# Attention and mixture of experts on one core: weight sums and a remainder moved to other places of the schedule, a scratch tile of their own, some copies on ScalarE

## The chip, the cores and the metric

The program runs on one core of one Trainium2 chip. The metric is the device time of one execution in microseconds (us); medians and ranges are over the executions of a job. TensorE is called PE in the profile, VectorE DVE, ScalarE ACT, GpSimd POOL, SyncE SP; "SPq" rows are transfers that the sync engine issues. The time in such a row is that of the issue; the data land later (tile 1's outputs 3.3 to 3.9 us after their issue in the changed kernel).

## The reference

```python
# q, k, v: (batch 8, heads 8, positions 576, 64)
scores = 1 / np.sqrt(64) * np.matmul(q, k.transpose(0, 1, 3, 2))
ret = scores * Dmat                     # gamma_h ** (i - j) for i >= j, else 0
attn = np.matmul(ret, v)
x = attn.transpose(0, 2, 1, 3).reshape(4608, 512)
p = domain_probs / (domain_probs.sum(-1, keepdims=True) + 1e-09)
for e in range(4):                      # w1[e]: 512 x 1024, w2[e]: 1024 x 512
    out += p[:, e:e+1] * (np.maximum(x @ w1[e], 0) @ w2[e])
```

## The kernel before

The 4608 tokens are worked in nine tiles of 512. A batch has 576 positions: four chunks of 128 and a remainder of 64. Tile 0 uses ordinary matmuls for x @ w1; from tile 1, expert 1 on, a "fast" product takes seven block products in place of eight, and for this it needs sums of weight blocks (per expert) and sums of token blocks (per tile). Attention of the next batches is woven into the same instruction streams.

Weight sums, all on VectorE, with two scratch tiles out of the ring `tmp`, which the token sums on GpSimd use too:

```python
def weight_sums(e):
    s = ssum[e] = wpool.tile([128, 3, 2, HF], BF16, tag=f"ws_{e}", name="wsum")
    ...
    for kc in range(2):
        def first(...):
            t[1] = tpool.tile([128, HF], FP32, tag="tmp", name="tmp")
            nc.vector.tensor_tensor(t[1], a21, a22, op=ADD)
        def second(...):
            t[2] = tpool.tile([128, HF], FP32, tag="tmp", name="tmp")
            nc.vector.tensor_tensor(t[2], t[1], a11, op=SUB)
        jobs += [first, second,
                 lambda ...: nc.vector.tensor_copy(s[:, 0, kc], t[1]),
                 lambda ...: nc.vector.tensor_copy(s[:, 1, kc], t[2]),
                 lambda ...: nc.vector.tensor_tensor(s[:, 2, kc], a12, t[2], op=SUB)]
        late.append(...)        # a21 <- a11 - a21, in place
```

Tile 0 is a list of 56 numbered groups of matmuls; `at(g, ...)` puts work behind group g in program order (T: transposes of queries and keys, S: scores, O: attention outputs, x: their copies into the token tile):

```python
at(39, T(0) of batch 1); at(40, S(0), masks); ...; at(47, O(3), x(3))      # shortened
at(48, narrow, lambda: [f() for f in token_sums(1)],
       lambda: [a1().cast_rem(n, nc.gpsimd) for n in "kqv"])
at(50, lambda: a1().Trem())
at(52, lambda: (a1().Srem(), a1().Srem_mask()))
at(54, lambda: (a1().Orem(), a1().x(NCH, nc.vector)))
sums_at(1, 17); sums_late(1, 22); sums_at(0, 23)
sums_at(2, 33); sums_late(2, 38); sums_at(3, 48); sums_late(3, 53)
for g in range(49, 56):
    at(g, lambda: pool(1, 2))           # two GpSimd items of batch 2 and later
```

From then on a loop over tiles and experts emits `up_fast` twice for each expert. It has four gaps each time, and a gap takes four matmuls of the second product, up to two GpSimd items and one TensorE item of the attention chain. The output tiles `acc` are four buffers, so tile 2's first expert writes (on ScalarE) where tile 1's outputs have to be gone; and all input loads, transposes and outputs are issued by the sync engine in program order:

```python
apool = tc.tile_pool(name="apool", bufs=NSUB)                              # NSUB = 4
def evacuate(po, ns, cols):
    if e == 0:
        nc.scalar.activation(a, po, Copy, scale=pe)
    else:
        nc.vector.scalar_tensor_tensor(a, po, pe, a, op0=MULT, op1=ADD)
    if e == E - 1:
        eng = nc.scalar if cols.start else nc.sync
        eng.dma_start(out=out[...], in_=a)
...
# in the chain of batch b, after its remainder's casts:
add("POOL", lambda: (load_chunk(b + 1, 2), load_chunk(b + 1, 3), load_rem(b + 1)))
```

## Time and profile before

| | before |
|---|---|
| time, median (lowest to highest) | 559.34 us (558.02 to 560.03) |
| TensorE busy | 535.0 us of 558.7 |
| two long TensorE waits | 6.8 and 4.75 us |
| first fast product starts at | 108.37 us |

The page of the kernel before: busy time, the granted clock of TensorE in tenths in 40 slices of the span, and the chain that ended last. Apart from the first and the last slice, TensorE is under 90% busy only in slices 5 to 8, 56 to 112 us.

```profile
span 558.7 us, 10485 instructions
...
PE 535.0 (96%) x4133; PEld 334.5 (60%) x4206; DVE 266.3 (48%) x427; ACT 251.6 (45%) x450; POOL 225.9 (40%) x321
...
PE   8999876799999999999999999999999999999997
...
PEclk9999979799999999999999999999999999999999
...
PE 91%; DVE 5%; issue 1%; POOL 1%; DMA 1%; SPq 0%; POOLq 0%; DVEq 0%
```

The waits of TensorE, longest first in total: who waited, for whom, total, times, longest.

```profile
PE ptr L306 <- POOL qrb L275: 6.8, 1, 6.8
PE s L315 <- DVE qkT L298: 4.8, 1, 4.8
```

The first stall, in the timeline of the kernel before (start, duration, engine, line, operation; in brackets the idle time and what ended it). VectorE works off weight sums of expert 2 before it copies the transposed tile, and TensorE waits for that copy. The first line is the same operation as the second, at a time when GpSimd is idle. (Four of expert 2's sums here, under GpSimd's casts, took 1.2 to 1.5 us, the others 0.4 to 1.0.)

```profile
50.89 0.41 DVE L553 CAST wsum<-tmp 128x512 bf16<-128x512 f32 x1
...
62.04 1.29 DVE L553 CAST wsum<-tmp 128x512 bf16<-128x512 f32 x1
...
65.76 1.53 DVE L546 TENSOR_TENSOR tmp<-wt 128x512 f32<-128x512 bf16 x1
...
70.34 2.01 DVE L556 TENSOR_TENSOR wt<-wt 128x512 bf16<-128x512 bf16 x2
72.27 0.41 DVE L298 COPY qkT<-ptc 128x512 bf16<-128x512 bf16 x1
72.73 0.61 PE L315 MATMUL s<-qkT 64*128 64x128 bf16 x8 [4.75 <-DVE qkT L298]
```

The second stall. GpSimd idles for 15.69 us, then works off the token sums of tile 1 and only after them casts the remainder of batch 1.

```profile
91.55 1.15 POOL L566 TENSOR_TENSOR tmp<-xT 128x512 f32<-128x512 bf16 x1 [15.69 <-DVE xT L233]
...
98.88 1.48 POOL L275 TENSOR_TENSOR qrb<-raw_qr,gq 64x512 bf16<-64x512 f32 x1
...
100.42 0.39 PE L306 MATMUL ptr<-ident,qrb 64*128 64x64 bf16 x4 [6.80 <-POOL qrb L275]
```

And the clock after each of them, in stretches of 2 us: stretch, busy time of each engine, granted clock, mean share of the DMA engines, GB/s. The clock is at half while TensorE works again; by the stretches after these it is full at about 77.9 and 105.2 us, that is 5.2 and 4.8 us after the work begins.

```profile
72.00:74.00 2.00, 1.27 (x17) 0.77 (x17) 1.26 (x3) 0.26 (x1) 2.00 (x3) 0.50 1.02 213
74.00:76.00 2.00, 2.00 (x11) 1.14 (x10) 0.72 (x3) 0.94 (x3) 0.86 (x2) 0.50 0.93 168
...
102.00:104.00 2.00, 1.79 (x5) 0.67 (x5) 2.00 (x2) 0.60 (x1) 2.00 (x3) 0.50 0.53 125
```

### The profile page before, as it was taken

The page shows a single profiled execution, that of the slowest core. Times are in us where ns is not written, and L with a number is a line of the kernel's source. Part 1 is how long each engine was busy: PE and PEld are TensorE (multiplying, and loading weights), DVE is VectorE, ACT ScalarE, POOL GpSimd, SP SyncE. Part 2 cuts the span into 40 slices and gives each one's busy share as a digit, 9 for nine tenths or more (in the row PEclk, how much of TensorE's full clock was granted, in tenths as well). Part 3 has the DMA queues.
Part 4 walks back from the last instruction along what each step waited for, and adds up shares of the span by engine and source line. Part 5 has one row for each costly group of instructions (what it writes and reads, how often), then busy time and mean ns, then how long its engine had stood idle before and what let it go on. Part 6 is the DMA issues. An engine that isn't in the chain of part 4 may idle for free.

```text
span 558.7 us, 10485 instructions
## 1 busy us (share of the span) xinstructions
PE 535.0 (96%) x4133; PEld 334.5 (60%) x4206; DVE 266.3 (48%) x427; ACT 251.6 (45%) x450; POOL 225.9 (40%) x321
## 2 busy tenths in 40 slices
PE   8999876799999999999999999999999999999997
PEld 3644443466666666666666666666666666666664
DVE  6618864945554455434443545344524442443343
ACT  3453232264445544454446344644464446445541
POOL 6601534947928836842264635510510320100000
PEclk9999979799999999999999999999999999999999
DMA  9999995589399396595028901200100010001002
GB/s 237 194 205 200 215 205 90 142 154 168 57 178 200 78 186 91 131 192 81 2 95 141 170 11 76 49 1 1 73 5 0 2 76 1 0 17 61 2 1 76
DMA packets 148817, 53.98 MB, mean 97 GB/s; under 512 B 130684, under 2 KB 143228, under 8 KB 148768
## 3 DMA queue, kind: packets, MB, share of 16 engines
q1 hardware_dynamic: 141296, 44.79, 40.0%
q0 software_dynamic: 7328, 8.39, 8.9%
q8 instruction: 33, 0.54, 0.4%
q14 instruction: 16, 0.13, 0.1%
q10 hardware_dynamic: 144, 0.13, 0.1%
HBM read 45.16 MB, written 9.44 MB: 98 GB/s over the span
## 4 chain that ended last, share of the span: by engine, by line
PE 91%; DVE 5%; issue 1%; POOL 1%; DMA 1%; SPq 0%; POOLq 0%; DVEq 0%
PE po L519 43%; PE upP L583 20%; PE upR L583 10%; PE ph L478 5%; PE upQ L583 5%; PE oc L356 2%; PE s L315 2%; PE kvp L326 1%; PE oc L359 1%; DVE wt L556 1%; DMA raw_q<-in_q_dram 1%; DVE wsum L555 0%; PE warm_out L153 0%; DVE acc L509 0%; DVE xT L233 0%
## 5 line engine op out<-in xcount | busy, mean ns | idle before, releaser
L519 PE MATMUL po<-wt,hT 128*128 128x512 bf16 (+1 forms) x1093 | 278.7, 377 | 3.6 <-issue 0.3
L519 PEld LDWEIGHTS <-hT 128*128 128x128 bf16 x1160 | 113.2, 98 | 81.3
L604 POOL TENSOR_SCALAR hT<-hT 128x512 bf16<-128x512 bf16 x62 | 38.1, 614 | 211.5 <-DVE hT L603 210.7
L509 DVE SCALAR_TENSOR_TENSOR acc<-po,probs,acc 128x512 f32<-128x512 f32 (+1 forms) x109 | 80.9, 742 | 79.0 <-PE po L519 75.3
L583 PEld LDWEIGHTS <-wt 128*128 128x128 bf16 x992 | 91.3, 98 | 35.9 <-issue 0.2
L595 DVE TENSOR_TENSOR upR<-upP,m 128x512 f32<-128x512 f32 x62 | 43.4, 699 | 126.9 <-PE upP L583 126.9
L583 PEld LDWEIGHTS <-wsum 128*128 128x128 bf16 x744 | 72.6, 98 | 21.1
L583 PE MATMUL upP<-tsum,wt 128*128 128x256 bf16 x496 | 74.8, 273 | 0.1
L603 DVE TENSOR_TENSOR hT<-upP,m 128x512 bf16<-128x512 f32 x62 | 42.9, 692 | 55.7 <-PE upP L583 54.2
L598 ACT ACTIVATE hT<-upQ 128x512 bf16<-128x512 f32 x62 | 37.0, 597 | 69.1 <-PE upQ L583 69.1
L608 ACT ACTIVATE hT<-upR 128x512 bf16<-128x512 f32 x62 | 37.0, 597 | 54.3 <-PE upR L583 54.3
L612 ACT ACTIVATE hT<-upP 128x512 bf16<-128x512 f32 x62 | 37.0, 597 | 48.7 <-PE upP L583 47.1
L589 ACT ACTIVATE upQ<-upP 128x512 f32<-128x512 f32 x62 | 36.1, 583 | 46.2 <-PE upP L583 46.1
L320 DVE TENSOR_TENSOR sT<-s,tri 128x512 bf16<-128x512 f32 x56 | 37.9, 682 | 9.3 <-PE s L315 9.3
L494 ACT ACTIVATE hT<-ph 128x512 bf16<-128x512 f32 x40 | 23.5, 597 | 41.6 <-PE ph L478 40.8
L478 PE MATMUL ph<-xT,wt 128*128 128x512 bf16 (+3 forms) x174 | 39.7, 377 | 0.6 <-issue 0.4
L583 PE MATMUL upP<-xT,wt 128*128 128x256 bf16 x248 | 37.4, 273 | 0.0
L583 PE MATMUL upQ<-xT,wt 128*128 128x256 bf16 x248 | 37.2, 273 | 0.0
L583 PE MATMUL upP<-tsum,wsum 128*128 128x256 bf16 x248 | 37.2, 273 | 0.0
L583 PE MATMUL upR<-xT,wsum 128*128 128x256 bf16 x248 | 37.2, 273 | 0.0
L583 PE MATMUL upR<-tsum,wsum 128*128 128x256 bf16 x248 | 37.2, 273 | 0.0
L591 ACT ACTIVATE m<-upR 128x512 f32<-128x512 f32 x62 | 36.7, 592 | 0.0
(110 smaller groups left out, 457.5 us busy)
## 6 DMA issues: line engine op xcount, KB each, us to landing
out_dram<-acc SPq DMA_DIRECT2D x35, 256.0 KB, 2.1
raw_k<-in_k_dram SPq DMA_DIRECT2D x32, 256.0 KB, 4.8
raw_q<-in_q_dram SPq DMA_DIRECT2D x32, 256.0 KB, 5.1
raw_v<-in_v_dram SPq DMA_DIRECT2D x32, 256.0 KB, 5.2
wt<-in_moe_w_dram POOLq DMA_DIRECT2D x6, 1024.0 KB, 25.2
wt<-in_moe_w_dram POOLq DMA_DIRECT2D x4, 512.0 KB, 6.8
raw_kr<-in_k_dram SPq DMA_DIRECT2D x8, 128.0 KB, 5.1
raw_qr<-in_q_dram SPq DMA_DIRECT2D x8, 128.0 KB, 4.6
```

The source lines that it names most:

```text
L320: nc.vector.tensor_tensor(self.sT[c][:, j], self.s[c][j], tri[:, :].unsqueeze(1).to_broadcast([128, NP, C]), op=MULT)
L478: nc.tensor.matmul(ph[:, ts], lhsT=w1_sb[e][:, dc, fc * 128:(fc + 1) * 128], rhs=xts[nt][:, dc, ts], start=(dc == 0), stop=(dc == NDC - 1))
L509: nc.vector.scalar_tensor_tensor(a, po, pe, a, op0=MULT, op1=ADD)
L519: nc.tensor.matmul(po, lhsT=hT[:, fc, ns * 128:(ns + 1) * 128], rhs=w2_sb[e][:, fc, d:d + w], start=(fc == 0), stop=(fc == NFC - 1))
L583: nc.tensor.matmul(ps[:, l], lhsT=wa(kc)[:, f:f + 128], rhs=xa(kc), start=(start and l == 0 and kc == 0), stop=(kc == 1), skip_group_check ...
L591: nc.scalar.activation(m5, R_, Copy)
L595: nc.vector.tensor_tensor(R_, P, m5, op=ADD)
L598: nc.scalar.activation(hT[:, lo, t0], Q, Relu)
L603: nc.vector.tensor_tensor(h22, P, m5, op=ADD)
L604: nc.gpsimd.tensor_scalar(h22, h22, float("inf"), 0.0, op0=MIN, op1=MAX)
L608: nc.scalar.activation(hT[:, lo, t1], R_, Relu)
L612: nc.scalar.activation(hT[:, hi, t0], P, Relu)
```

## The change

The intent is to take both stalls away: expert 2's sums where VectorE has time, the remainder's casts where GpSimd idles, and the remainder's matmuls and half of expert 3's sums in the fast loop of tile 1. The weight sums get a scratch tile of their own, worked in place, and for experts 0 and 1 ScalarE makes the copies. Batch 2's chain now has to wait for the remainder of batch 1 (`first`). The diff, cut to its core (left out are the new places of the sums of experts 0 and 1, the queue `extra` for the other half of expert 3's, and a move of batch 0's last remainder step from group 36 to 34):

```diff
+        def copy(o, i):
+            if e < 2:
+                nc.scalar.activation(o, i, Copy)
+            else:
+                nc.vector.tensor_copy(o, i)
...
+            t = tpool.tile([128, HF], FP32, tag="wsum", name="wt", bufs=1)
...
+                nc.vector.tensor_tensor(t, a21, a22, op=ADD)
+                copy(s[:, 0, kc], t)
...
-            add("POOL", lambda: A.cast_rem("k", g), **({"PE": P} if n else {}))
+            add("POOL", lambda: A.cast_rem("k", g), **({"PE": P} if n else {"first": 1}))
...
-                add("PE", lambda: A.S(c), DVE=V + v, ACT=X + x, later=(b, c))
+                add("PE", lambda: A.S(c), DVE=V + v, ACT=X + x, later=(b, c), **({} if n else {"first": 2}))
...
+                elif k == "first":
+                    ok = len(rem1) < n
...
-    at(48, narrow, lambda: [f() for f in token_sums(1)], lambda: [a1().cast_rem(n, nc.gpsimd) for n in "kqv"])
-    at(50, lambda: a1().Trem())
-    at(52, lambda: (a1().Srem(), a1().Srem_mask()))
-    at(54, lambda: (a1().Orem(), a1().x(NCH, nc.vector)))
+    at(46, lambda: [a1().cast_rem(n, nc.gpsimd) for n in "kqv"])
+    at(48, narrow, lambda: [f() for f in token_sums(1)])
+    rem1 = {3: lambda: a1().Trem(), 5: lambda: (a1().Srem(), a1().Srem_mask()),
+            7: lambda: (a1().Orem(), a1().x(NCH, nc.vector))}     # by gap of the loop
...
-    sums_at(2, 33)
-    sums_late(2, 38)
-    sums_at(3, 48)
-    sums_late(3, 53)
+    sums_at(2, 26, 27, 28, 30, 31, 32)
+    sums_late(2, 33, 34)
+    sums_at(3, 48, 50, 52)              # the other half goes into the loop's windows
     for g in range(49, 56):
-        at(g, lambda: pool(1, 2))
+        at(g, lambda: pool(1, 1))
```

More of the change, by code (lines that the diff above doesn't have):

```diff
@@ L541, in weight_sums, with second @@
             a11, a12, a21, a22 = w[:, kc, :HF], w[:, 2 + kc, :HF], w[:, kc, HF:], w[:, 2 + kc, HF:]
-            t = {}
+            t = tpool.tile([128, HF], FP32, tag="wsum", name="wt", bufs=1)
             def first(kc=kc, a21=a21, a22=a22, t=t):
-                t[1] = tpool.tile([128, HF], FP32, tag="tmp", name="tmp")
-                nc.vector.tensor_tensor(t[1], a21, a22, op=ADD)
-            def second(a11=a11, t=t):
-                t[2] = tpool.tile([128, HF], FP32, tag="tmp", name="tmp")
-                nc.vector.tensor_tensor(t[2], t[1], a11, op=SUB)
-            jobs += [first, second,
-                     lambda kc=kc, t=t: nc.vector.tensor_copy(s[:, 0, kc], t[1]),
-                     lambda kc=kc, t=t: nc.vector.tensor_copy(s[:, 1, kc], t[2]),
-                     lambda kc=kc, t=t, a12=a12: nc.vector.tensor_tensor(s[:, 2, kc], a12, t[2], op=SUB)]
+                nc.vector.tensor_tensor(t, a21, a22, op=ADD)
+                copy(s[:, 0, kc], t)
+            def second(kc=kc, a11=a11, t=t):
+                nc.vector.tensor_tensor(t, t, a11, op=SUB)
+                copy(s[:, 1, kc], t)
+            jobs += [first, second, lambda kc=kc, t=t, a12=a12: nc.vector.tensor_tensor(s[:, 2, kc], a12, t, op=SUB)]
             late.append(lambda a11=a11, a21=a21: nc.vector.tensor_tensor(a21, a11, a21, op=SUB))
@@ L793 @@
     at(31, a0.Srem, a0.Srem_mask)
-    at(36, a0.Orem, lambda: a0.x(NCH, nc.vector))
+    at(34, a0.Orem, lambda: a0.x(NCH, nc.vector))
     at(25, begin1)
@@ L806, in narrow, with sums_at, sums_late @@
         turn.update(at=0)
-    at(48, narrow, lambda: [f() for f in token_sums(1)], lambda: [a1().cast_rem(n, nc.gpsimd) for n in "kqv"])
-    at(50, lambda: a1().Trem())
-    at(52, lambda: (a1().Srem(), a1().Srem_mask()))
-    at(54, lambda: (a1().Orem(), a1().x(NCH, nc.vector)))
+    at(46, lambda: [a1().cast_rem(n, nc.gpsimd) for n in "kqv"])
+    at(48, narrow, lambda: [f() for f in token_sums(1)])
+    rem1 = {3: lambda: a1().Trem(), 5: lambda: (a1().Srem(), a1().Srem_mask()),
+            7: lambda: (a1().Orem(), a1().x(NCH, nc.vector))}
     late = {}
-    def sums_at(e, g, n=2):
+    def sums_at(e, *gs):
         def start():
             state["jobs"], late[e] = weight_sums(e)
-        at(g, start)
-        for i in range(10):
-            at(g + i // n, lambda i=i: state["jobs"][i]())
-    def sums_late(e, g):
-        at(g, lambda: [f() for f in late[e]])
-    sums_at(1, 17)
-    sums_late(1, 22)
-    sums_at(0, 23)
-    sums_at(2, 33)
-    sums_late(2, 38)
-    sums_at(3, 48)
-    sums_late(3, 53)
+            extra.extend(state["jobs"][len(gs):])
+        at(gs[0], start)
+        for i, g in enumerate(gs):
+            at(g, lambda i=i: state["jobs"][i]())
+    def sums_late(e, *gs):
+        for i, g in enumerate(gs):
+            at(g, lambda i=i: late[e][i]())
+    sums_at(1, 16, 17, 17, 18, 19, 19)
+    sums_late(1, 20, 20)
+    sums_at(0, 20, 21, 21, 22, 23, 24)
+    sums_at(2, 26, 27, 28, 30, 31, 32)
+    sums_late(2, 33, 34)
+    sums_at(3, 48, 50, 52)
     for g in range(49, 56):
-        at(g, lambda: pool(1, 2))
+        at(g, lambda: pool(1, 1))
     head += [up_classical(0, 1), down_groups(0, 0), down_groups(0, 1), up_classical(0, 2), down_groups(0, 2),
@@ L847 @@
     turn.update(po=0)
-    extra += late[0]
-    before = (1, 0)
+    extra += late[3] + late[0]
+    before, gaps = (1, 0), 0
     for nt, e in [(nt, e) for nt in range(1, n_nt) for e in range(E)][1:]:
@@ L857, in gap @@
         def gap():
+            nonlocal gaps
+            gaps += 1
             for _ in range(4):
@@ L863, in gap @@
             pool(nt, 2)
+            rem1.pop(gaps, int)()
             chain.emit("PE", nt)
@@ L881 @@
             front.pop(0)()
+        while len(extra) > {(1, 1): 9, (1, 2): 9, (1, 3): 2}.get((nt, e), 0):
+            extra.pop(0)()
         for g in range(2):
```

## The prediction

> **What bounds the kernel.** TensorE: busy 535.0 of 558.7 us (96%, busy table), and the chain of waits is 91% TensorE. After about 112 us it is busy 99% (stretch table), so nothing is to be won there. Its idle time sits in two stalls of the first 110 us (waits of TensorE):
>
> 1. 4.75 us, 67.98 to 72.73 us: the first score matmuls of batch 1 wait for VectorE's copy of the transposed queries. VectorE has these weight sums of expert 2 queued ahead of the copy, from 60.05 us on (timeline), mixed with evacuations. They take 1.2 to 1.5 us each there, against 0.4 to 0.7 us at 49 to 55 us, because GpSimd casts batch 1 at the same time. (The Trainium skill, "SBUF — State Buffer", "Who interferes with whom", says such a VectorE instruction and a GpSimd one block each other; this trace agrees, with those numbers.)
> 2. 6.80 us, 93.6 to 100.42 us: the transposes of batch 1's remainder wait for GpSimd, which casts it (97.88 to 100.36) only after the token sums of tile 1 (91.55 to 97.9). GpSimd was idle from 75.9 to 91.5.
>
> Each stall drops the clock to 0.50 for about 5 us (granted clock by stretch; 128x512 matmuls go from 0.216 to 0.43 us apart). The Trainium skill, "TensorE: Matmul & The Clock Gate", "Part 1: The HAM clock gate", names both the half rate and the recovery after about 3.4 us of work; here it took nearer 5. That costs about 2.5 us per stall. A further 0.5 us is a wait for the remainder's mask at 107 us.
>
> **What the change does.** TensorE's work is the same, in another order.
> - Expert 2's sums move forward to 50-57 us, where VectorE has no evacuations and GpSimd is nearly idle. The first stall goes.
> - The remainder is cast before the token sums, in GpSimd's idle time, and its matmuls move into the gaps of tile 1's fast loop. The second stall goes; the token sums hide behind about 7 us of expert 0's matmuls.
> - Eight copies (0.4-0.8 us) of experts 0 and 1 go to ScalarE, which is 45% busy; the in-place scratch tile frees the sums from the token sums' tile (two 2.7 us VectorE waits).
> - Batch 2's scores begin four gaps later. Replaying the schedule, tile 2's token sums are still emitted about three gaps (5 us) before they are needed.
>
> **The sum.** Stalls 4.75 + 6.80 + 0.5 = 12.0; clock about 4.7; total 16.7. As a cross-check, the stretch 67.98-79.66 holds about 4.5 us of matmuls at full clock and 93.6-108.37 about 5.3, the same total. Costs that I expect: expert 0's second copy stands ahead of an activation evacuation on ScalarE while VectorE is late, at about 51 us (0.3-1 us); in tile 1's first fast group, expert 3's sums delay one VectorE addition (about 0.6 us, slowed by GpSimd). So 559.3 - 16.7 + 1.4 = 544.0 us. Range 540.5 to 548.0. Faster by over 2%: 0.91; within 2%: 0.08; slower: 0.01.
>
> **What would show it.** No TensorE wait over 1.5 us between 25 and 115 us; granted clock 1.00 there; TensorE busy about 530 us (fewer half-rate matmuls); expert 2's sums at about 0.7 us each; the first fast group starts near 92 us instead of 108.4; GpSimd casts the remainder at about 76-80 us.
>
> **What would make it wrong.** A new stall over about 3 us would drop the clock again: ScalarE blocked behind a weight-sum copy near 51 us, expert 3's sums with GpSimd's token sums and casts at 84-100 us, or GpSimd's late clamp of hT in tile 1 (my slack: about 6 us). Or batch 1's casts, paced by DMA until 76 us, become the next limit once stall 1 is gone (slack 1-3 us).

## The result, and the profile after

The changed kernel took 550.79 us (median of 4, 550.58 to 552.11) beside 559.68 us for the kernel before (558.02 to 560.78): a ratio of 0.9849, 95% interval 0.9819 to 0.9878. That is faster, but by 1.5%, outside the range. (A ratio is the mean time of one kernel's fast runs over that of the other's of the same rounds, so it is not quite the ratio of the medians.)

The page of the changed kernel. The low digits of slices 5 to 8 are gone; new ones stand in the twelfth and thirteenth slices.

```profile
span 548.9 us, 10483 instructions
...
PE 531.3 (97%) x4133; PEld 332.9 (61%) x4206; DVE 259.0 (47%) x419; ACT 255.7 (47%) x458; POOL 224.1 (41%) x321
...
PE   7999999999978999999999999999999999999997
...
PEclk9999999999997999999999999999999999999999
...
PE 92%; DVE 2%; DMA 2%; issue 1%; POOL 1%; SPq 0%; ACT 0%; DVEq 0%; ACTq 0%
```

The longest wait of TensorE in the changed kernel, and the longest that is left between 25 and 115 us:

```profile
PE upP L587 <- ACT upQ L593: 5.7, 1, 5.7
...
PE ph L478 <- ACT hT L494: 0.4, 1, 0.4
```

Up to there the forecast came true. Expert 2's sums run in GpSimd's quiet time at 0.43 to 0.71 us, and the remainder is cast from 76.2 us on. The first fast product starts at 89.75 us in place of 108.37 us. In the timeline of the changed kernel:

```profile
50.49 0.43 DVE L544 CAST wsum<-wt 128x512 bf16<-128x512 f32 x1
...
66.14 0.43 DVE L298 COPY qkT<-ptc 128x512 bf16<-128x512 bf16 x1 [2.92 <-PE ptc L296]
...
76.20 1.04 POOL L275 TENSOR_TENSOR krb<-raw_kr,gk 64x512 bf16<-64x512 f32 x1
...
89.75 0.60 PE L587 MATMUL upP<-xT,wt 128*128 128x256 bf16 x4
```

The kernel is thus 18.6 us ahead at the start of the loop. But from there to the end it takes 459.15 us (548.9 - 89.75) where the kernel before took 450.3 (558.7 - 108.37). About 0.8 us of the 8.8 is the remainder's matmuls, which moved into the loop. The rest is a new stall at 161 us and the half clock after it. The timeline of the changed kernel there, VectorE first (it finishes the second and the last output block of tile 1), then the sync queue, ScalarE and TensorE:

```profile
143.27 0.75 DVE L509 SCALAR_TENSOR_TENSOR acc<-po,probs,acc 128x512 f32<-128x512 f32 x1 [1.53 <-PE po L519]
...
151.02 0.75 DVE L509 SCALAR_TENSOR_TENSOR acc<-po,probs,acc 128x512 f32<-128x512 f32 x1 [1.00 <-PE po L519]
...
151.37 1.77 SPq L512 DMA_DIRECT2D out_dram<-acc  x1
153.19 0.43 SPq L109 DMA_DIRECT2D raw_k<-in_k_dram  x1
...
160.90 1.25 SPq L123 DMA_DIRECT2D raw_vr<-in_v_dram  x2
162.25 1.51 SPq L512 DMA_DIRECT2D out_dram<-acc  x3
...
165.62 0.69 ACT L507 ACTIVATE acc<-po,probs 128x512 f32<-128x512 f32 x1 [6.90 <-DMA out_dram<-acc]
166.21 0.59 ACT L593 ACTIVATE upQ<-upP 128x512 f32<-128x512 f32 x1
...
166.85 1.01 PE L587 MATMUL upP<-tsum,wsum 128*128 128x256 bf16 x4 [5.72 <-ACT upQ L593]
```

Read from below: TensorE waits for ScalarE to empty an accumulator bank; ScalarE stands before an earlier instruction, which writes tile 2's second `acc` buffer; that buffer still holds tile 1's second output block. VectorE had finished that block at 144.0 us (143.27 + 0.75), but its transfer left at 162.25 us, because the input loads of batch 4 stood ahead of it in the sync queue. Of these 18.2 us the last ten loads are 9.0; the rest is the first six loads, two transposes and tile 1's first output, which stay ahead of it in the runs defer and half too. The wait list names only ScalarE; one has to go two steps up to find a transfer. And the clock follows; it is full again at about 171.5 us, so it costs about 2.3 us:

```profile
166.00:168.00 2.00, 1.15 (x6) 0.82 (x6) 0.03 (x1) 1.31 (x3) 0.00 (x0) 0.50 0.88 163
168.00:170.00 2.00, 2.00 (x8) 0.75 (x6) 1.26 (x2) 0.60 (x1) 0.00 (x0) 0.50 0.52 104
```

In the kernel before the same loads also stood ahead of tile 1's outputs, but they started 7.35 us before VectorE took up tile 1's last block (162.86 against 170.21) and the last of them was issued 1.9 us after that block was done (172.84 against 170.96); in the changed kernel they start 2.2 us after it (153.19 against 151.02). Before, ScalarE had a wait for an output too, and TensorE none for it:

```profile
162.86 0.58 SPq L109 DMA_DIRECT2D raw_k<-in_k_dram  x1
...
170.21 0.75 DVE L509 SCALAR_TENSOR_TENSOR acc<-po,probs,acc 128x512 f32<-128x512 f32 x1 [1.01 <-PE po L519]
...
172.93 1.51 SPq L512 DMA_DIRECT2D out_dram<-acc  x3
...
175.79 0.69 ACT L507 ACTIVATE acc<-po,probs 128x512 f32<-128x512 f32 x1 [1.86 <-DMA out_dram<-acc]
```

### The profile page after: what moved, and what is told of

The parts are those of the page before. It is cut to its first block, busy times and chain, and to the rows that moved or that the text cites. A ratio compares the mean times of both kernels' runs of the same rounds, so it can differ in the third digit from the quotient of the medians.

```text
span 548.9 us, 10483 instructions
## 1 busy us (share of the span) xinstructions
PE 531.3 (97%) x4133; PEld 332.9 (61%) x4206; DVE 259.0 (47%) x419; ACT 255.7 (47%) x458; POOL 224.1 (41%) x321
## 4 chain that ended last, share of the span: by engine, by line
PE 92%; DVE 2%; DMA 2%; issue 1%; POOL 1%; SPq 0%; ACT 0%; DVEq 0%; ACTq 0%
PE po L519 43%; PE upP L587 20%; PE upR L587 10%; PE ph L478 6%; PE upQ L587 5%; PE oc L356 2%; PE s L315 2%; DMA raw_q<-in_q_dram 1%; PE oc L359 1%; PE kvp L326 1%; DVE sT L447 1%; DMA out_dram<-acc 1%; POOL km L267 0%; PE ptc L296 0%; DVE qm L398 0%
## 5 line engine op out<-in xcount | busy, mean ns | idle before, releaser
L478 PE MATMUL ph<-xT,wt 128*128 128x512 bf16 (+3 forms) x175 | 35.8, 355 | 0.6 <-ACT hT L494 0.4
L267 POOL TENSOR_TENSOR km<-raw_k,gk 128x512 bf16<-128x512 f32 x28 | 30.2, 1078 | 12.0 <-DMA raw_k<-in_k_dram 9.3
```

Source lines behind the costliest of these rows:

```text
L478: nc.tensor.matmul(ph[:, ts], lhsT=w1_sb[e][:, dc, fc * 128:(fc + 1) * 128], rhs=xts[nt][:, dc, ts], start=(dc == 0), stop=(dc == NDC - 1))
```

## The experiments

Theory A: the outputs wait in the sync queue behind batch 4's loads, since batch 2's chain, and with it every later load, now lags four gaps further behind the loop. Rival B: the DMA engines are simply full there, wherever the output stands. Rival C: the wait is only labelled so. Rival D: the earlier start of the loop alone brings the stall about, with either half of the change. Eleven runs were made, of nine new kernels (again is the changed kernel, defer5 is defer once more), all with correct results. Each job ran the kernel before on the same chip; the medians of before were 558.81, 559.52 and 558.69 us for the three jobs.

### outq: outputs of tile 1 on ScalarE's queue

```diff
-                eng = nc.scalar if cols.start else nc.sync
+                eng = nc.scalar if cols.start or nt == 1 else nc.sync
```

> The changed kernel with one edit: the four output transfers of tile 1 are issued by ScalarE's own DMA queue in place of the shared sync queue. Theory A (the new 5.7 us stall of TensorE near 161 us is ScalarE waiting for an accumulator tile whose output transfer stands in the sync queue behind batch 4's input loads): ScalarE's 6.9 us wait for the output and the half-clock stretch after it go; no TensorE wait over 2 us after 110 us; about 543 us (541.5 to 545). Rival B (the DMA engines are saturated by the loads there, whatever queue the output uses): ScalarE still waits 5 us or more for the output, about 550 us. Rival C (the wait is only labelled so; ScalarE is held by something else of the change): about 550 us.

Measured: 547.26 us (546.70 to 549.02), ratio 0.9792 (0.9734 to 0.9850). ScalarE's wait for an output is gone, and TensorE has a new wait of 2.5 us:

```profile
PE s L315 <- ACT xT L231: 2.5, 1, 2.5
...
153.99 0.60 ACT L612 ACTIVATE hT<-upR 128x512 bf16<-128x512 f32 x1 [5.58 <-DVE ksum L346]
```

ScalarE now has to stop until it may issue a transfer (one of its instructions waited 5.58 us at 154 us, behind the third output). So 543 us was missed by 4 us: the run trades one in-order engine for another. But it removes the old wait without touching the loads, which still ran in the sync queue (154.15 to 164.9 us) as the outputs landed, 2.5 to 4.6 us after their issue; that speaks against B. The Trainium skill, "DMA: Bandwidth & Descriptors", section "Issuing engines are not separate DMA queues", says that issuing from several engines saves only sequencer time, usually small beside the transfer. Here it was not small: it took away ScalarE's wait of 6.9 us, and in spite of ScalarE's own stop the kernel gained about 3.5 us (550.79 against 547.26, medians of two jobs).

### spare: another buffer for tile 2's second accumulator

```diff
-            acc[nt] = [apool.tile([128, Dm], FP32, tag="acc", name="acc") for _ in range(NSUB)]
+            acc[nt] = [tpool.tile([128, Dm], FP32, tag="wsum", name="acc", bufs=1) if (nt, ns) == (2, 1)
+                       else apool.tile([128, Dm], FP32, tag="acc", name="acc") for ns in range(NSUB)]
```

(One more buffer in `apool` does not fit into SBUF: the program does not build. The scratch tile of the weight sums is free by then and of the same size.)

> The changed kernel, but tile 2's second accumulator tile is put into the 2 KB scratch of the weight sums, free by then, so it needs no output of tile 1; the third then waits for the output that the second waited for before, about 3.9 us later in the schedule. Theory A: the 6.9 us wait shrinks to about 2.8 us, the TensorE stall to about 1.5 us (ScalarE had about 1.2 us of slack), the clock stays full; 544 to 546 us. If the accumulator's reuse is not the cause: about 550.5 us.

Measured: 544.53 us (543.48 to 544.85), ratio 0.9732 (0.9685 to 0.9779). ScalarE's wait is 3.1 us, now at the third buffer, TensorE's 1.0 us, and the clock stays at 1.00 in the profile. The loads and outputs were as before: only the need for the buffer moved, and the stall went with it. Rival C falls.

### defer: batch 4's last loads behind tile 1's outputs

```diff
-                add("POOL", lambda: (load_chunk(b + 1, 2), load_chunk(b + 1, 3), load_rem(b + 1)))
+                def loads():
+                    load_chunk(b + 1, 2), load_chunk(b + 1, 3), load_rem(b + 1)
+                add("POOL", lambda: held.append(loads) if b == 3 else loads())
...
+        if (nt, e) == (2, 1):
+            held.pop()()
```

> The changed kernel, but the last input loads of batch 4 (8 transfers, about 9 us of the sync queue) are issued after tile 1's outputs instead of before three of them. Theory A: the outputs leave at about 151 us, the stall goes, about 543 us (541.5 to 545). Rival B (bandwidth): the bytes are the same and close by, so a wait of several us remains, 547 us or more.

Measured: 543.91 us (542.73 to 545.39), ratio 0.9726 (0.9677 to 0.9775). No wait for an output is left. The same bytes move, a few us later: with the outputs first they do no harm. Rival B falls. The outputs were issued at 154.22 us, not at about 151: six loads and two transposes are still ahead of them. (These are ten transfers, six of chunks and four of the remainder; the expectation called them eight.)

### sums_only: the weight-sum half of the change alone

The kernel before with the new `weight_sums`, the new places of the sums, and the emptying of `extra` in the loop; the remainder and the chain as before. (The move of batch 0's remainder step from group 36 to 34 is in neither half.)

> The kernel before with only the weight-sum half of the change (expert 2 earlier, expert 3 later, ScalarE copies, own scratch). The first stall (4.75 us) and its half clock go, the second stays at 6 to 7 us. Theory A, with the lag of batch 2's chain behind tile 1's loop (it comes from the remainder half) as the reason for the late loads: no new stall near 160 us, so 559.5 - 7.2 = about 552.3 us (551 to 554). Rival D (the late stall comes from any earlier start of the fast loop): a ScalarE wait for the output of 4 us or more shows here too, and the time is 556 us or more.

Measured: 554.99 us (554.14 to 558.35), ratio 0.9934 (0.9877 to 0.9990). The first stall is gone, the second is there (6.3 us). ScalarE waits 3.65 us for an output, TensorE 1.6 us after it. The time is 2.7 us above my 552.3. TensorE's new waits in the profile are 2.8 us together: this one and three of 0.4 us, at 101, 134 and 136 us. ScalarE's wait is 1.8 us longer than the 1.86 us of the kernel before, so part of the late stall appears already here: the slack before was thin, and rival D holds for a part, since this half alone eats some of it.

### rem_only: the remainder half alone

The kernel before with `cast_rem` at 46, `rem1`, the gates `first` and `pool(1, 1)`; the weight sums as before.

> The kernel before with only the remainder half of the change (cast ahead of the token sums, remainder's matmuls in the gaps of tile 1's loop, batch 2's chain four gaps later, half the GpSimd items in the head). The second early stall goes (-9.7 us with its clock and the mask wait), the first stays. Theory A (the lag of batch 2's chain against tile 1's loop puts batch 4's loads ahead of tile 1's outputs): the ScalarE wait for the output of 5 to 8 us and the TensorE stall of 4 to 7 us near 170 us appear here too: 556.5 to 559.5 us, so this half gives back nearly all that it wins. Rival D (it takes the earlier start of the loop from both halves): a ScalarE wait under 4 us, 550 to 553 us.

Measured: 568.75 us (567.15 to 570.19), ratio 1.0181 (1.0138 to 1.0224): slower than the kernel before. The TensorE waits of this run:

```profile
PE upP L583 <- DVE upR L595: 10.7, 1, 10.7
PE upP L583 <- ACT upQ L589: 4.7, 1, 4.7
PE s L315 <- DVE qkT L298: 4.5, 1, 4.5
```

The late stall came as theory A wanted it (ScalarE waits 5.9 us for an output, TensorE 4.7), with the first stall still in place: the lag makes it, by itself. The loop is not ahead here (VectorE takes up tile 1's last block at 171.03 us, before at 170.21), so rival D has no part in it. But I had forgotten another thing. Without the second stall TensorE reaches the loop at 96.4 us while VectorE still has all but the first of expert 3's sums before it, held up by the shared ring and slowed by GpSimd, and until 110.00 us it does not get to the loop's first addition:

```profile
96.65 1.51 DVE L550 TENSOR_TENSOR tmp<-tmp,wt 128x512 f32<-128x512 f32 x1 [2.73 <-POOL tsum L568]
...
110.00 0.69 DVE L595 TENSOR_TENSOR upR<-upP,m 128x512 f32<-128x512 f32 x1
...
110.75 1.04 PE L583 MATMUL upP<-tsum,wt 128*128 128x256 bf16 x4 [10.71 <-DVE upR L595]
```

The remainder half needs the other one: the second stall had also been the time in which VectorE did expert 3's sums.

### before_defer: the late loads in the kernel before

> Control: the kernel before with only the late issue of batch 4's last loads, after tile 1's outputs. There the ScalarE wait for the output was 1.86 us and TensorE did not wait for it. Theory A: the ScalarE wait goes and the time stays, ratio 0.997 to 1.003. If late loads are a gain by themselves, 0.99 or lower, and the result of the run defer says less.

Measured: 560.27 us (558.56 to 561.05), ratio 1.0022 (0.9974 to 1.0070). ScalarE's wait is gone, the time the same. Late loads are no gain by themselves.

### defer_dve: copies of experts 0 and 1 back on VectorE, on top of defer

```diff
-            if e < 2:
+            if e < 0:
```

> The changed kernel with deferred loads, and with the eight copies of experts 0 and 1 back on VectorE (own scratch and new places kept). The 0.4 to 0.8 us TensorE wait for ScalarE's activation near 50 us goes; VectorE has about 3.4 us more to do before 53 us, which may delay expert 2's sums and the remainder of batch 0. If the ScalarE copies matter: 1 us or more slower than 543.9. I expect 543 to 545, within the noise.

Measured: 544.65 us (544.06 to 544.75), ratio 0.9748 (0.9712 to 0.9784), against 0.9726 for defer in another job; the intervals overlap. The wait of TensorE for ScalarE near 50 us is gone and two waits for VectorE, 1.2 us together, took its place. By these waits the copies on ScalarE are worth 1 us or less; the times do not settle whether anything.

### defer_shared: the scratch back in the shared ring, on top of defer

```diff
-            t = tpool.tile([128, HF], FP32, tag="wsum", name="wt", bufs=1)
+            t = tpool.tile([128, HF], FP32, tag="tmp", name="wt")
```

> The changed kernel with deferred loads, and with the weight sums' scratch back in the ring of two that the token sums use. Expert 3's sums then wait for GpSimd's token sums (two waits of 2.7 us in the kernel before) and run into tile 1's first fast group: VectorE late there, TensorE stall of 1 to 4 us at 93 to 97 us; 545 to 548 us. If the own scratch tile is not needed: 543.9 within 1 us.

Measured: 546.09 us (545.05 to 546.33), ratio 0.9773 (0.9736 to 0.9810). TensorE waits 1.8 and 0.4 us for VectorE in tile 1's first fast group, as expected. In the same job that is 1.4 us more than defer_dve (medians), which differs in the copies too. The intervals of the two ratios overlap, so the waits carry this verdict more than the times do.

### again, defer5 and half: the stall's size, and a dose

Three kernels on one chip with five rounds: the changed kernel unedited, defer once more, and half, in which three of the ten transfers stay ahead of the outputs (seven go behind; the expectation called them five):

```diff
-                    load_chunk(b + 1, 2), load_chunk(b + 1, 3), load_rem(b + 1)
-                add("POOL", lambda: held.append(loads) if b == 3 else loads())
+                    load_chunk(b + 1, 3), load_rem(b + 1)
+                add("POOL", lambda: (load_chunk(b + 1, 2), held.append(loads) if b == 3 else loads()))
```

> The changed kernel once more, unedited, beside the next two on one chip: 550 to 552 us, ScalarE's wait for the output of 6 to 8 us, TensorE's stall of 5 to 6.5 us and a half clock after it.

> The changed kernel with batch 4's last loads (8 transfers) after tile 1's outputs, as before, more rounds: 543 to 545 us. The difference to the changed kernel on this chip should be the stall (5.7 us) and about 2.2 us of half clock, 7 to 8 us. If it is under 5 us, something else of the late stretch is in it.

> Dose: only the last five of these transfers (chunk 3 and the remainder) go after tile 1's outputs, three stay ahead. Theory A: the three take about 3 us of the queue, outputs leave near 156 us and land near 158.5, when ScalarE needs the second tile at about 158.7; a ScalarE wait of 0 to 2.5 us, TensorE stalled 0 to 1.3 us, 543.5 to 545.5 us. A rival in which the order alone, not the queue's time, matters: half of the stall stays, about 547 us.

| run | transfers ahead | ACT wait for an output | PE stall | median (range), us | ratio (95%) |
|---|---|---|---|---|---|
| again | 10 | 6.5 | 5.4 | 551.48 (550.56 to 552.57) | 0.9877 (0.9843 to 0.9911) |
| half | 3 | 0.4 | 0 | 543.72 (542.94 to 544.06) | 0.9735 (0.9699 to 0.9771) |
| defer5 | 0 | 0 | 0 | 543.02 (542.42 to 543.81) | 0.9725 (0.9692 to 0.9758) |

The sync queue of half, and ScalarE's write of the second buffer: the three loads take 3.15 us of the queue (152.73 to 155.88), the output still lands in time.

```profile
152.73 1.20 SPq L109 DMA_DIRECT2D raw_k<-in_k_dram  x1
...
155.88 1.84 SPq L512 DMA_DIRECT2D out_dram<-acc  x3
...
160.03 0.69 ACT L507 ACTIVATE acc<-po,probs 128x512 f32<-128x512 f32 x1 [0.36 <-DMA out_dram<-acc]
```

The changed kernel and defer5 differ by 8.46 us. The profile of again accounts for it: 5.4 us of stall, and then TensorE at half clock from 167.15 to about 173.2 us (the granted clock of 172 to 174 us is 0.71), which is 6.0 us at half speed, or 3.0 us lost; together 8.4 us. In defer5 the row of the clock is nines throughout, and the chain that ended last is 96% TensorE:

```profile
PE 535.0 (99%) x4206; PEld 332.9 (61%) x4206; DVE 260.1 (48%) x419; ACT 256.0 (47%) x458; POOL 224.1 (41%) x321
...
PEclk9999999999999999999999999999999999999999
...
PE 96%; DVE 2%; DMA 1%; issue 0%; ACT 0%; SPq 0%; DVEq 0%
```

defer, half and spare all beat both kernels, defer by 2.75% against the kernel before (defer5); their intervals overlap.

## Why the prediction was wrong

What was right:

- **The two stalls and their clock.** Both went. Up to the loop the kernel won 18.6 us in its profile, some 0.8 of them only moved; in the six later profiles with the same first part the loop starts at 90.4 to 92.6 us, which is 15.8 to 18.0 us won. The prediction's 544.0 us is, within 1 us, what the change is worth without the late stall: defer measured 543.91 and 543.02 us.
- **Half clock after a stall.** The Trainium skill, "TensorE: Matmul & The Clock Gate", "Part 1: The HAM clock gate", gives half rate after an idle window of about 3.4 us. All runs agree, though no stall lay between 2.5 and 4.5 us to test the figure itself: those of 4.5 us and more were each followed by a half clock, and those of 2.5 (outq), 1.8 (defer_shared), 1.6 (sums_only) and 1.0 us (spare) left it at 1.00.
- **VectorE and GpSimd together.** Expert 3's first four two-input operations, under GpSimd's token sums, took 1.5 to 1.6 us in the changed kernel (L552 at 83.70: 1.60; the last two, under its casts, 0.93), 0.7 us when GpSimd was quiet, as the skill's "SBUF — State Buffer", "Who interferes with whom", has it.
- **The small cost near 51 us.** I estimated 0.3 to 1 us; TensorE waited 0.4 us for ScalarE.

What was wrong:

- **The step that failed** is this one: "Batch 2's scores begin four gaps later. Replaying the schedule, tile 2's token sums are still emitted about three gaps (5 us) before they are needed." The lag was right, and the token sums were in time. But I checked only this one consumer of the chain. The chain also issues the loads of later batches into the one queue that carries the outputs. With the lag, batch 4's last loads no longer begin 7.35 us before VectorE takes up tile 1's last block, but 2.2 us after it; and tile 2's `acc` needs those outputs gone. The missing term of the sum was 8.0 us in the changed kernel's profile (5.7 of stall, 2.3 of clock), 8.5 us by the times (again against defer5); with the two costs at 0.4 in place of 1.4 us, the sum then gives 551.0 us, beside 550.79 measured. My list of dangers named ScalarE, expert 3's sums, the clamp of hT and batch 1's casts, but no transfer behind 115 us, and my tests ended there: I had set the rest aside because the kernel before was 99% busy after 112 us. A stretch without waits is not a stretch with slack: the profile before showed a ScalarE wait of 1.86 us for an output there, and I did not ask what stood before it.
- **The 0.6 us in tile 1's first fast group** did not show: no TensorE wait is listed there.
- **"TensorE busy about 530 us"** agreed by accident (531.3). Both profiles lack 73 matmul records of 4206; with all records the changed kernel has 537.4 us (again), and defer5, without any half clock, 535.0. The sum of busy time was no test of this step.

Shown are: the order in the queue and the reuse of the buffer as the cause (defer, spare, half, and outq for the wait), the lag as enough to make it (rem_only), and the size. The timelines also say how much each half does. Against VectorE's last block of tile 1 the last loads begin 7.35 us early in the kernel before, 6.2 us early in sums_only (156.20 against 162.42), level with it in rem_only (171.04 against 171.03) and 2.2 us late in the changed kernel. So the remainder half moves them by 7.4 us and the weight-sum half by 1.1; about 1 us of the 9.5 belongs to neither alone. Left open is why the weight-sum half, with no lag of gaps, moves them at all: the loop there starts 9.3 us earlier than before (99.03 against 108.37 us), but I have not separated what of the loads' own pace goes into it.

## What to carry to other kernels

When a change shifts one stream of work against another, list everything that the shifted stream issues, transfers into shared in-order queues too, and for each the consumer and its slack; a wait that costs nothing in the profile before is the place where slack is nearly used up. Outputs whose buffers are soon to be rewritten belong ahead of loads that nobody needs yet. And before a stall is removed, ask which other engine was using that time: rem_only took one away and got a longer one.

## What the Trainium skill lacked or had wrong

- "TensorE: Matmul & The Clock Gate", Part 1, gives about 3.4 us of work until full clock, and around 4 us, half a microsecond either way, for one measured run. Here it took longer: 5.2 and 4.8 us after the two stalls of the kernel before, about 4.6 us of work after the late stall in the changed kernel (166.85 to about 171.5 us) and 6.0 us in the run again. The page calls its window free-running, which may be why; no run here tests it.
- "DMA: Bandwidth & Descriptors", "Issuing engines are not separate DMA queues", treats the choice of the issuing engine as a small matter of sequencer time. It does not say there how long a transfer can stand behind others in one issuing engine's order: in the changed kernel an output ready at 144.0 us left at 162.25 us, putting loads behind outputs was worth 8.5 us, and outputs on another engine about 3.5.
- The pages give bandwidths and the cost of small descriptors, but I found none with the time that such loads occupy the issuing queue; the runs show about 9 us for ten of them, 1.9 MB (153.19 to 162.15 us in the changed kernel), with the DMA engines busy.
